# Attention, two mixtures of experts on one core: whole tiles in the gathering, gate values behind places, and a new order of steps in the second mixture

## The chip, the core and the metric

One core of a Trainium2 chip runs the whole program. The time is the device time of one execution in microseconds, and the median over several runs counts. Five engines work side by side: TensorE (matrix products), VectorE, ScalarE, GpSimd and SyncE, called PE, DVE, ACT, POOL and SP in the profile. SyncE here only issues transfers, in order.

## The reference

```python
def reference(**kwargs):
    attn_out = _attn_ref(q, k, v, s)                      # (2, 8, 576, 64): causal, with a decay bias from cumsum(max(s, 0))
    x = attn_out.transpose(0, 2, 1, 3).reshape(1152, 512)
    x = _moe_ref(x, w_gate, w1, w2, capacity=288)         # first mixture: each token to its best of 8 experts
    return _moe2_ref(x, w_gate2, w1b, w2b)                # second: greedy by logit, 144 tokens per expert
```

The bias of a score is `-(cum[i] - cum[j])`, clipped at zero, before the softmax. In the first mixture a token goes to the expert with the largest logit and is scaled by its softmax probability; an expert takes its first 288 tokens. In the second, pairs of token and expert are taken in falling order of their logits, and each expert is full at 144 tokens. An expert computes `relu(x @ w1) @ w2` with w1 of 512 x 1024 and w2 of 1024 x 512.

## The kernel before, in words

The order of the work is written out by hand: no scheduler moves an instruction, and each engine takes its own in program order. Weights and activations are split into a high half in 16 bits and a low half (the rest), so that three products of halves stand for one in 32 bits.

**Attention** runs over 16 heads (two batches of eight), in pairs. A loop `m` from -7 to 18 (line 745) runs a software pipeline: in one turn head `m` gets its exponentials (`E0` to `E3`, line 515) and the halves `ph` and `pl` of its probabilities (`P0`, `P1`, line 536), head `m - 1` its products with v (`V0` to `V2`, `R0` to `R2`), head `m + 3` its row maxima (`M0` to `D3`, lines 464 and 481) and the reference level that is subtracted in the exponent (`G0` and `G1`, lines 488 and 492), pair `m / 2 + 3` its q in 16 bits (`QS`, line 419, whose copy `QD` is line 423). Names and order of a turn are the two lists `ORDER` (line 740). `ENG` (line 391) says by name which engine does a copy: D for VectorE, A for ScalarE, P for GpSimd. The helpers `copied` and `less` carry lines 398, 400, 402 and 411 for all of them. When a pair has its output, `X1` (line 593) makes its two halves in the rows XR, `X` transposes them, `XE` copies them out and `XG` multiplies them with the gate's weights; `LG` adds the logits.

**The gate.** `gate(b)` (line 653) takes the logits of a batch: the maximum, which expert it is (a one-hot `OH`), the exponentials for the gate value, a matmul with a triangle of ones that counts each token's place at its expert, then `sl`, the row of the token in the list `xd` in DRAM, and a scatter of the rows by GpSimd (line 688). For the second batch `slf` is its place within the first expert. The first expert's input is not read back from DRAM only: `first_pe0` (line 628) puts the first batch's part into four banks, and `first_pe1` (line 634) adds the second batch's tokens by a product of XR with one-hots `oh0` of places (line 637: five VectorE operations, one for each 128 tokens, the last of 64). Forty matmuls (line 642) give XA, copied out by ScalarE and VectorE in turn (line 644). `warmer` (line 648) issues matmuls whose results are not used; `WARM` says how many.

**First mixture.** From line 1274 on, eight experts in an order of their sizes. Weights come from DRAM by SP (line 128), are split by ScalarE (line 160, high) and VectorE or GpSimd (line 164, low), in steps put between the matmuls. `split_next` does one quarter of a matrix. Four such quarters, the first expert's first matrix, are split during attention's end: `SPA` (line 698) gives one after each of the turns 13 to 15, line 819 one more, and two of their low halves are GpSimd's (`POOL0`). The load of the second expert's first matrix goes into the same buffer, when all four are split.

**Second mixture.** `phases` (line 1686) finds in up to seven rounds which tokens the next full expert gets, in steps that end with `yield`, while the experts already known are computed. The strings `FIRST` and `THEN` (line 1871) say what stands between an expert's matmuls at each of 22 places: `h` and `l` a high and a low half of a weight split, `w` the next step of `phases`, `s` and `t` the transposes of the next expert's input (`spread`, line 1407), `0` and `1` the two halves of the previous expert's output. `checks` (line 1760) makes sums over the result, from which the kernel decides at the end whether to route again.

## Time and profile before

| | |
|---|---|
| median of 3 runs | 489.27 us (487.54 to 490.25) |
| the profiled execution | 487.02 us, its span 485.2 us |
| PE busy | 413.0 us, 85% of the span |
| DVE busy | 321.1 us, 66% |
| ACT busy | 244.4 us, 50% |
| POOL busy | 190.3 us, 39% |
| DRAM | 81.42 MB read, 14.59 MB written, 198 GB/s over the span |

The span runs from the first to the last instruction; what lies around it makes up the rest of the execution. Attention fills the span up to about 150 us, the first mixture 163 to 280, the choice of the second mixture's tokens up to 326, the second mixture the rest. A share of the whole span is a mean over these, so the rows below are by stretch.

### The profile page before, as it was taken

How to read it: one execution, taken by the hardware profiler on the slowest of the kernel's cores; microseconds unless marked ns; L12 is line 12 of the kernel's file. 1: busy time of each engine (PE TensorE's matmuls, PEld its weight loads, DVE VectorE, ACT ScalarE, POOL GpSimd, SP SyncE). 2: the span in 40 equal slices, each digit the busy share in tenths (PEclk: the TensorE clock that was granted, in tenths of full speed). 3: DMA queues.
4: the chain of work that ended last, by engine and by line, in shares of the span. 5: the costliest groups of instructions: out<-in, count | busy, mean ns of one | idle time of the engine just before them, and what ended most of it. 6: DMA issues, size and time to landing. Idle time of an engine off the chain costs nothing. (4 is left out here: it accounts for less than half of the span.)

```text
span 485.2 us, 13714 instructions
## 1 busy us (share of the span) xinstructions
PE 413.0 (85%) x5227; PEld 380.5 (78%) x5227; DVE 321.1 (66%) x949; ACT 244.4 (50%) x441; POOL 190.3 (39%) x299
## 2 busy tenths in 40 slices
PE   1679999977987999999999985649999999998980
PEld 1557778766774799999999985639899899998980
DVE  6799999995865357777778935458773763653300
ACT  3466777743662246545667604225456456454420
POOL 3595667756743503212322700432233322332211
PEclk9999999987987699999999988657999999999995
DMA  8787889749903689999996910449999769689001
GB/s 174 167 202 168 206 194 223 139 139 313 263 3 127 204 238 387 341 345 391 343 344 139 179 25 7 133 121 273 362 333 340 233 192 353 230 287 309 15 26 29
DMA packets 94405, 103.09 MB, mean 212 GB/s; under 512 B 56136, under 2 KB 63304, under 8 KB 94323
## 3 DMA queue, kind: packets, MB, share of 16 engines
q1 hardware_dynamic: 88931, 91.85, 65.3%
q0 software_dynamic: 4192, 9.91, 6.3%
q8 instruction: 45, 0.74, 0.6%
q10 hardware_dynamic: 1200, 0.30, 0.3%
q14 instruction: 37, 0.30, 0.2%
HBM read 81.42 MB, written 14.59 MB: 198 GB/s over the span
## 5 line engine op out<-in xcount | busy, mean ns | idle before, releaser
L164 DVE TENSOR_TENSOR wl<-wf,wh 128x1024 bf16<-128x1024 f32 x62 | 74.7, 1222 | 19.7 <-ACT wh L160 17.5
L160 ACT ACTIVATE wh<-wf 128x1024 f16<-128x1024 f32 x64 | 65.8, 1050 | 12.3 <-DMA wf<-in_moe_w_dram 12.3
L906 PE MATMUL A<-xt,wl 128*128 128x144 f16 (+4 forms) x288 | 61.0, 235 | 0.0
L905 PE MATMUL A<-xt,wh 128*128 128x144 f16 (+4 forms) x288 | 61.0, 235 | 0.0
L904 PE MATMUL A<-xt,wh 128*128 128x144 f16 (+4 forms) x288 | 61.0, 235 | 0.0
L1074 POOL DMA_INDIRECT x2d<-xo,tix x16 | 26.3, 1646 | 81.7 <-DVE l L1090 33.9
L961 PE MATMUL C<-h,wf 128*128 128x160 f32 (+7 forms) x544 | 58.3, 269 | 0.0
L906 PEld LDWEIGHTS <-wl 128*128 128x128 bf16 x512 | 51.8, 101 | 2.6 <-issue 2.6
L904 PEld LDWEIGHTS <-wh 128*128 128x128 f16 x512 | 51.9, 101 | 1.4 <-PE pM L642 1.4
L905 PEld LDWEIGHTS <-wh 128*128 128x128 f16 x512 | 51.7, 101 | 0.9 <-issue 0.4
L534 ACT ACTIVATE pf<-pE,XB 128x512 f32<-128x512 f32 (+4 forms) x80 | 36.9, 514 | 19.7 <-PE pE L529 15.5
L1815 POOL DMA_INDIRECT out_dram<-x2f,tok x14 | 15.7, 1121 | 66.9 <-ACT h L915 37.5
L411 POOL TENSOR_TENSOR pl<-pf,ph 128x512 f16<-128x512 f32 x30 | 35.2, 1186 | 14.3 <-DVE ph L400 12.6
L961 PEld LDWEIGHTS C<-h,wf 128*128 128x128 f32 x256 | 36.2, 190 | 0.0
L1795 PE MATMUL C<-h,wf 128*128 128x144 f32 x256 | 35.3, 290 | 0.0
L485 DVE CUSTOM_DVE_ANT_0 junk<-pM,cb 128x128 f16<-128x128 f32 (+4 forms) x80 | 32.1, 428 | 3.7 <-PE pM L475 3.6
L473 PE MATMUL pM<-al,ar 128*128 128x128 f16 (+2 forms) x96 | 27.4, 326 | 8.0 <-DVE rm L485 5.1
L1795 PEld LDWEIGHTS C<-h,wf 128*128 128x128 f32 x256 | 32.4, 190 | 0.0
L1399 POOL DMA_INDIRECT xg<-x2d,tok x16 | 22.6, 1411 | 22.1 <-PE A L1117 7.2
L557 PE MATMUL pog<-vf,pf 128*128 128x65 f32 x180 | 30.0, 291 | 0.0
L904 PE MATMUL C<-xt,wh 128*128 128x144 f16 x128 | 25.7, 232 | 0.0
L905 PE MATMUL C<-xt,wh 128*128 128x144 f16 x128 | 25.7, 232 | 0.0
(404 smaller groups left out, 1186.9 us busy)
## 6 DMA issues: line engine op xcount, KB each, us to landing
wf<-in_moe_w_dram SPq DMA_DIRECT2D x128, 512.0 KB
xd<-zero SPq DMA_DIRECT2D x18, 257.0 KB
cb<-cumd SPq DMA_DIRECT2D x16, 288.0 KB
x2d<-zero SPq DMA_DIRECT2D x9, 260.5 KB
kf<-in_k_dram SPq DMA_DIRECT2D x16, 128.0 KB
vf<-in_v_dram SPq DMA_DIRECT2D x16, 128.0 KB
qf<-in_q_dram SPq DMA_DIRECT2D x14, 128.0 KB
bl<-al SPq DMA_DIRECT2D x16, 72.0 KB
```

What stands on the lines that cost most here:

```text
L160: nc.scalar.activation(hi, src, AF.Copy)
L164: (nc.gpsimd if i == 0 and (0, part) in POOL0 else nc.vector).tensor_sub(lo, src, hi)
L411: (nc.gpsimd if ENG[name][i % 2] == "P" else nc.vector).tensor_sub(o, x, y)
L473: nc.tensor.matmul(o, AR[m][:, t * P:(t + 1) * P], AL[m][:, j0:j1], start=True, stop=not diag)
L485: nc.vector.tensor_tensor_reduce(junk[:w, :j1 - j0], o, CB[m][:w, j0:j1], 1.0, r if t == 4 and j0 == 0 else -3e38, OP.add, OP.max, r)
L534: nc.scalar.activation(d, o, AF.Exp, bias=x, scale=2.0 ** -13)
L557: nc.tensor.matmul(o, pf[:, c:c + P], VF[n % 4][:, j, h], start=False, stop=j == t)
L904: nc.tensor.matmul(ph[:, g], wh[:, c, fs], xt[:, c], start=c == 0, stop=False)
L905: nc.tensor.matmul(ph[:, g], wh[:, c, fs], xt[:, 4 + c], start=False, stop=False)
L906: nc.tensor.matmul(ph[:, g], wl[:, c, fs], xt[:, c], start=False, stop=c == 3)
L961: nc.tensor.matmul(py[:, g], a[:, f, d], b[:, f], start=k == 0, stop=k == len(terms) - 1)
L1795: nc.tensor.matmul(py[:, g], a[:, f, d], b[:, f], start=k == 0, stop=k == len(terms) - 1)
```

## The change

In attention's loop the scaling of the row maxima (`q_dve0`) goes from VectorE to ScalarE, with the constant MAGIC as a bias from a tile; the subtraction in `q_dve1` goes from VectorE to GpSimd, and MAGIC is now in `refb`, which VectorE writes; the copy `QD` goes from GpSimd to VectorE. At attention's end: `X1` of pair 6 runs at the end of turn 14 and no longer in turn 15, turn 16 begins with `X` and `XE`, two splits go from before the gate into `first_pe1`, all low halves are VectorE's, the gathering takes five whole tiles (the last filled up with zeros), gate values and the scatter come after the places and one-hots, and the numbers of warming matmuls and their places differ. In the second mixture the strings and one `yield` differ.

```diff
--- before.py
+++ after.py
@@ -78,7 +78,6 @@
     wsp0 = ctx.enter_context(tc.tile_pool(name="wsp0", bufs=1))
     WSP = [tuple(wsp0.tile([P, 4096], t, name=f"{n}{i}") for n, t in (("wh", F16), ("wl", BF16))) for i in range(2)]
     WS = {}
-    POOL0 = ((0, 1), (0, 3))
     ROWS = ('DA', 'DD')
 
     FILL = ". ff ffff ff rf f f rff ff . . . r rf ff fffffff"
@@ -161,7 +160,7 @@
 
     def split_lo(i, part):
         src, hi, lo = split_parts(i, part)
-        (nc.gpsimd if i == 0 and (0, part) in POOL0 else nc.vector).tensor_sub(lo, src, hi)
+        nc.vector.tensor_sub(lo, src, hi)
 
     def split_w(i, part):
         split_hi(i, part)
@@ -327,7 +326,10 @@
 
     g1 = sp.tile([P, S], F32, name="g1")
     XB = ap.tile([P, NT, NH], F32, name="XB")
+
     refb = ap.tile([P, NH, G], F32, name="refb")
+    magic = ap.tile([P, 1], F32, name="magic")
+    nc.vector.memset(magic, MAGIC)
 
     def groups():
         nc.vector.tensor_scalar(g1[64:96], gi[64:96], 0.0, -1024.0, op0=OP.is_ge, op1=OP.mult)
@@ -357,7 +359,7 @@
             nc.tensor.matmul(pr[:, h], selc[:, h:h + 1].to_broadcast([64, P]), refh, start=True, stop=True)
         nc.scalar.activation(XB[:, :4], pb[:, :4], AF.Copy, scale=2.0 ** -13)
         nc.scalar.activation(XB[:64, 4], pb[:64, 4], AF.Copy, scale=2.0 ** -13)
-        nc.scalar.activation(refb, pr, AF.Copy)
+        nc.vector.tensor_scalar(refb, pr, MAGIC, None, op0=OP.add)
 
 
     wgh = const.tile([P, 4, 2, E], F16, name="wgh")
@@ -389,7 +391,7 @@
     later = []
 
     ENG = dict(KL="DD", QL="DD", BR="DD", AL="AA", AR="AA", XE0="AA", XE1="AA", XH="AA",
-               XL="PP", NH="PP", NL="PP", KH="AA", QH="AA", QD="PP", last="DD", PH0="DD", PH1="DD", PL0="PP", PL1="PP",
+               XL="PP", NH="PP", NL="PP", KH="AA", QH="AA", QD="DD", last="DD", PH0="DD", PH1="DD", PL0="PP", PL1="PP",
                VS="DD", VL="PP", VH="AA")
 
     def copied(name, i, o, x, scale=None):
@@ -486,17 +488,16 @@
                                            r if t == 4 and j0 == 0 else -3e38, OP.add, OP.max, r)
 
     def q_dve0(m):
+
         rm = RMS[m % 4]
-        nc.vector.tensor_scalar(rm[:, :NT], rm[:, :NT], 2.0 ** -10, MAGIC, op0=OP.mult, op1=OP.add)
+        nc.scalar.activation(rm, rm, AF.Identity, bias=magic, scale=2.0 ** -10)
 
     def q_dve1(m):
         n, h, b, hh = heads(m)
-        rm = RMS[m % 4]
         qb = QB[n % 3]
         ng = aw.tile([P, NT, G], F32, name="ng")
-        nc.vector.scalar_tensor_tensor(ng, rm[:, :NT, None].to_broadcast([P, NT, G]), MAGIC,
-                                       refb[:, m, None, :].to_broadcast([P, NT, G]),
-                                       op0=OP.subtract, op1=OP.subtract)
+        nc.gpsimd.tensor_tensor(ng, RMS[m % 4][:, :NT, None].to_broadcast([P, NT, G]),
+                                refb[:, m, None, :].to_broadcast([P, NT, G]), OP.subtract)
         copied("NH", m, qb[:, :, h, 64:64 + G], ng)
         less("NL", m, qb[:, :, h, 96:96 + G], ng, qb[:, :, h, 64:64 + G])
 
@@ -631,35 +632,46 @@
             pxa.append(pool.tile([P, 512], F32, name=name)[:, :2 * CA].rearrange("p (c n) -> p c n", c=2))
             nc.tensor.matmul(pxa[k], ident, XA0[:, 2 * k:2 * k + 2], start=True, stop=False, skip_group_check=True)
 
+    oh0s = []
+
+    def first_ones():
+        oh0 = aw.tile([P, NT, 2, 2 * D], F16, name="ka").rearrange("p t h d -> p t (h d)")[:, :, :CA]
+        nc.gpsimd.memset(oh0[64:, 4], 0.0)
+        oh0s.append(oh0)
+
     def first_pe1():
-        oh0 = aw.tile([P, NT, 2, 2 * D], F16, name="ka").rearrange("p t h d -> p t (h d)")[:, :, :CA]
+        oh0 = oh0s[0]
         for t, w in TW:
             nc.vector.tensor_scalar(oh0[:w, t], iota0[:w], slf[:w, t:t + 1], None, op0=OP.is_equal)
+        gate_rows(1)
         for k in range(4):
             for c in range(2):
                 d = 2 * k + c
-                for t, w in TW:
-                    nc.tensor.matmul(pxa[k][:, c], XRP[1][:w, 1, t, d * P:(d + 1) * P], oh0[:w, t], start=False,
+                for t in range(NT):
+                    nc.tensor.matmul(pxa[k][:, c], XRP[1][:, 1, t, d * P:(d + 1) * P], oh0[:, t], start=False,
                                      stop=t == NT - 1, skip_group_check=True)
             (nc.vector.tensor_copy if k % 2 else nc.scalar.copy)(XA[:, 2 * k:2 * k + 2], pxa[k])
-
-    WARM = (4, 4, 2, 2, 4, 4)
+            if k in (0, 2):
+                split_next()
+
+    WARM = (4, 4, 2, 2, 10, 8, 8)
 
     def warmer(k):
 
         for _ in range(WARM[k]):
             nc.tensor.matmul(pog[:, :256], ident, XRP[1][:, 0, 0, :256], start=True, stop=True)
+
+    gates1 = {}
 
     def gate(b):
         lg = LG[:, b]
         g = aw.tile([P, 5, NT], F32, name="gg")
         t3 = aw.tile([P, 3, NT, E], F32, name="gt3")
+        gates1[b] = g, t3
         bc = lambda a: a[:, :, None].to_broadcast([P, NT, E])
         nc.vector.reduce_max(g[:, 0], lg, axis=AX.X)
         nc.vector.tensor_tensor(t3[:, 0], lg, bc(g[:, 0]), OP.is_ge)
-        nc.vector.tensor_tensor(t3[:, 1], lg, bc(g[:, 0]), OP.subtract)
         nc.vector.tensor_tensor(t3[:, 0], t3[:, 0], erev[:, None, :].to_broadcast([P, NT, E]), OP.mult)
-        nc.scalar.activation(t3[:, 1], t3[:, 1], AF.Exp, scale=1.0 / (SX * SG))
         nc.vector.reduce_max(g[:, 1], t3[:, 0], axis=AX.X)
         nc.vector.tensor_tensor(OH[:, b, :4], t3[:, 0, :4], bc(g[:, 1])[:, :4], OP.is_equal)
         nc.vector.tensor_tensor(OH[:64, b, 4], t3[:64, 0, 4], bc(g[:, 1])[:64, 4], OP.is_equal)
@@ -672,18 +684,25 @@
         for t in range(NT - 1):
             mm.append((ones, OH[:, b, t, None, :].to_broadcast([P, NT - 1 - t, E]), t + 1))
         for i, (l, r, t) in enumerate(mm):
+            if b and i == b * NT:
+                warmer(4)
             nc.tensor.matmul(pr[:, t:], l, r, start=i == 0, stop=i == len(mm) - 1, skip_group_check=True)
-        nc.vector.reduce_sum(g[:, 2], t3[:, 1], axis=AX.X)
-        nc.vector.tensor_scalar(g[:, 2], g[:, 2], 1e-9, None, op0=OP.add)
-        nc.vector.reciprocal(xrf[:, b * NT:(b + 1) * NT, 0], g[:, 2])
+        nc.vector.tensor_tensor(t3[:, 1], lg, bc(g[:, 0]), OP.subtract)
+        nc.scalar.activation(t3[:, 1], t3[:, 1], AF.Exp, scale=1.0 / (SX * SG))
         nc.vector.tensor_tensor(t3[:, 2], pr, OH[:, b], OP.mult)
         nc.vector.reduce_sum(g[:, 3], t3[:, 2], axis=AX.X)
         nc.vector.tensor_scalar(g[:, 4], g[:, 3], float(CAP), 1e6, op0=OP.is_ge, op1=OP.mult)
         nc.vector.scalar_tensor_tensor(g[:, 3], g[:, 1], -float(CAP), g[:, 3], op0=OP.mult, op1=OP.add)
-        sl = const.tile([P, NT], I32, name=f"slot{b}")
         if b:
             nc.vector.scalar_tensor_tensor(slf, g[:, 3], e0off, g[:, 4], op0=OP.add, op1=OP.add)
+
+    def gate_rows(b):
+        g, t3 = gates1[b]
+        sl = const.tile([P, NT], I32, name=f"slot{b}")
         nc.vector.scalar_tensor_tensor(sl, g[:, 3], float(E * CAP), g[:, 4], op0=OP.add, op1=OP.add)
+        nc.vector.reduce_sum(g[:, 2], t3[:, 1], axis=AX.X)
+        nc.vector.tensor_scalar(g[:, 2], g[:, 2], 1e-9, None, op0=OP.add)
+        nc.vector.reciprocal(xrf[:, b * NT:(b + 1) * NT, 0], g[:, 2])
         for t, w in TW:
             i = nc.gpsimd.indirect_dma_start(
                 out=xd[:, :], out_offset=bass.IndirectOffsetOnAxis(ap=sl[:w, t:t + 1], axis=0),
@@ -695,7 +714,7 @@
     def rows_x(e, s0, N):
         return slice(e * CAP + s0, e * CAP + s0 + N) if isinstance(e, int) else bass.ds(e * CAP + s0, N)
 
-    SPA = {13: 1, 14: 1, 15: 1}
+    SPA = {13: 1, 14: 1}
 
 
     cnt = const.tile([P, E], F32, name="cnt")
@@ -786,13 +805,23 @@
                              ("L", 9, load_pair), ("LV", 6, load_v), ("XG", -4, lambda n: make("XG", x_pe, n)),
                              ("LG", -4, lambda n: use("XG", lg_add, n))):
             pair_task(name, off, f)
-        for name in ORDER[m % 2]:
+        names = ORDER[m % 2]
+        if m == NH:
+
+            names = ["X", "XE"] + [x for x in names if x not in ("X", "XE")]
+        for name in names:
+            if m == NH - 1 and name == "X1":
+                continue
             if name in tasks:
                 tasks[name]()
                 if m == NH and name in ("V2", "XG"):
                     warmer(name == "XG")
+        if m == NH - 2:
+            x1(NPAIR - 2)
+            first_ones()
         if "LG" in tasks and m == 2 * NP + 2:
             gate(0)
+            gate_rows(0)
             first_experts()
         if m == -5:
             references()
@@ -816,14 +845,13 @@
             nc.sync.dma_start_transpose(XA0, xd.bitcast(F16)[rows_x(order[0], 0, CA), :2 * DM])
         for _ in range(SPA.get(m, 0)):
             split_next()
-    split_next()
     first_pe0()
-    warmer(4)
     gate(1)
     pc = psT.tile([P, S], F16, name="pT").bitcast(F32)[:, :B * NT * E]
     nc.tensor.matmul(pc, ones, OH.rearrange("p b t e -> p (b t e)"), start=True, stop=True)
     warmer(5)
     first_pe1()
+    warmer(6)
     nc.vector.reduce_sum(cnt, pc.rearrange("p (c e) -> p e c", e=E), axis=AX.X)
     nc.vector.scalar_tensor_tensor(key, cnt, float(E), erev, op0=OP.mult, op1=OP.add)
     nc.vector.tensor_tensor(key, key, taken, OP.subtract)
@@ -1761,6 +1789,7 @@
 
         nc.gpsimd.tensor_tensor(chk[:, 0], own0[:, 0], own0[:, 0], OP.mult)
         nc.gpsimd.tensor_tensor(chk[:, 1, :CT], SL2, SL2, OP.mult)
+        yield
         nc.vector.reduce_sum(Q[:, 0, :E], chk[:, 0].rearrange("p t e -> p e t"), axis=AX.X)
         nc.vector.reduce_sum(Q[:, 1, :E], chk[:, 1, :CT].rearrange("p t e -> p e t"), axis=AX.X)
         nc.vector.reduce_sum(dbl[:, 0], BA0, axis=AX.X)
@@ -1868,8 +1897,8 @@
 
 
 
-    FIRST = "w h lw l . 0ww ww . . . . w . ww h . l h wst lh lw1 hll"
-    THEN = "w . . . 0 . . ww . w h l1w h wl . h l . swh tl l ."
+    FIRST = "w h wl l . w . w w w w . w . wh l w h st lh wl hll"
+    THEN = "w . . . 0 w w . w . h w1l h wl h . w l s tl h l"
     FIRST, THEN = (x.split() for x in (FIRST, THEN))
     next(work)
     pop_lo()
```

## Rows read from the trace of the kernel before

**Rows 1.** Busy time by stretch: length, busy us (instructions) per engine, clock, DMA share, GB/s
```profile
17.00:40.00 23.00, 15.85 (x166) 11.56 (x165) 22.04 (x73) 11.95 (x25) 17.85 (x61) 0.93 0.83 199
40.00:100.00 60.00, 57.21 (x818) 48.08 (x818) 59.55 (x199) 45.02 (x96) 40.50 (x49) 1.00 0.82 181
153.00:166.00 13.00, 11.20 (x69) 7.48 (x67) 4.51 (x22) 0.85 (x2) 8.03 (x20) 0.50 0.72 250
166.00:262.00 96.00, 96.00 (x1112) 95.04 (x1109) 69.60 (x126) 54.96 (x93) 24.60 (x33) 1.00 1.03 326
```

**Rows 2.** Groups of instructions by line and form, 40 to 100 us
```profile
L490 DVE TENSOR_SCALAR rm<-rm 128x5 f32<-128x5 f32 x9 | 9.3, 1036 | 0.0
...
L497 DVE SCALAR_TENSOR_TENSOR ng<-rm,refb 128x90 f32<-128x90 f32 x9 | 2.2, 244 | 0.1
...
L400 DVE CAST ph<-pf 128x512 f16<-128x512 f32 x17 | 9.1, 555 | 0.0
...
L400 POOL COPY qa<-qa 128x640 f16<-128x640 f16 x4 | 2.9, 717 | 0.0
...
L411 POOL TENSOR_TENSOR qb<-ng,qb 128x90 f16<-128x90 f32 x9 | 3.2, 352 | 0.7
```

**Rows 3.** Timeline at 74 us: start, us, engine, line, operation
```profile
74.68 1.16 POOL L411 TENSOR_TENSOR pl<-pf,ph 128x512 f16<-128x512 f32 x1 [0.43 <-DVE rs L568]
74.75 1.12 DVE L490 TENSOR_SCALAR rm<-rm 128x5 f32<-128x5 f32 x1
```

**Rows 4.** Timeline of attention's end, 138 to 163 us
```profile
138.35 1.90 DVE L411 TENSOR_TENSOR pl<-pf,ph 128x512 f16<-128x512 f32 x1
...
140.62 0.69 DVE L411 TENSOR_TENSOR pl<-pf,ph 128x512 f16<-128x512 f32 x1
...
142.56 1.27 PE L449 MATMUL pT<-ident,XR 128*128 128x128 f16 x10
...
150.17 1.51 DVE L659 TENSOR_TENSOR gt<-LG,gg 128x40 f32<-128x40 f32 x1
...
151.60 0.19 DVE L660 TENSOR_TENSOR gt<-LG,gg 128x40 f32<-128x40 f32 x1
...
153.97 0.94 DVE L637 TENSOR_SCALAR ka<-iota,slf 128x160 f16<-128x160 f16 x5
...
154.79 1.01 POOL L688 DMA_INDIRECT xd<-XR,slot  x1 [3.18 <-DVE ka L637]
...
155.01 0.64 PEld L642 LDWEIGHTS <-XR 64*128 64x128 f16 x5 [0.29 <-issue]
...
156.26 0.42 ACT L644 CAST XA<-pE 128x320 f16<-128x320 f32 x1 [4.20 <-PE pE L642]
...
162.00 0.49 DVE L644 CAST XA<-pM 128x320 f16<-128x320 f32 x1 [3.46 <-PE pM L642]
...
162.78 0.29 PE L904 MATMUL A<-XA,wh 128*128 128x160 f16 x1 [1.20 <-DVE cnt L827]
```

**Rows 5.** The two halves of a weight split (the page's groups), and SP's load at 151.65
```profile
L164 DVE TENSOR_TENSOR wl<-wf,wh 128x1024 bf16<-128x1024 f32 x62 | 74.7, 1222 | 19.7 <-ACT wh L160 17.5
...
L160 ACT ACTIVATE wh<-wf 128x1024 f16<-128x1024 f32 x64 | 65.8, 1050 | 12.3 <-DMA wf<-in_moe_w_dram 12.3
...
151.65 1.97 SPq L128 DMA_DIRECT2D wf<-in_moe_w_dram  x4
```

**Rows 6.** TensorE's waits from 326 us: us in total, times, longest us
```profile
PE A L1117 <- ACT xt L1420: 2.2, 3, 0.7
...
PE px L1394 <- DVE tot L1736: 1.1, 4, 0.3
...
PE px L1733 <- DVE own L1723: 0.8, 1, 0.8
...
PE D L905 <- DVE xt L1420: 2.3, 1, 2.3
```

**Rows 7.** The table load of ScalarE, all of the execution
```profile
L288 ACT ACT_TABLE_LOAD  x1: 1283/1283/1283, 2.5 to 2.5; - x1
```

## The prediction

> **What bounds the kernel now.** I read the busy time by stretch first [rows 1]. From 40 to 100 us, where nine heads of attention run, VectorE is busy 59.55 of 60 us and TensorE 57.21. Both look full, but only VectorE is: TensorE's short matmuls are counted with their latency, so its row overstates it. VectorE sets the pace there. It does so from 17 to 40 us as well, 22.04 of 23 us, where TensorE has 15.85. From 166 to 262 us, the first experts, TensorE is busy 96.00 of 96 us at the full clock and waits for nothing, so whatever starts this stretch sooner ends it sooner. In between lies the end of attention. From 153 to 166 us TensorE's granted clock is 0.50, which is 1.2 GHz, although the engine is counted busy for 11.20 of 13 us.
>
> Next come the lines of the stretch 40 to 100 [rows 2]. L490 is a VectorE operation on 5 numbers per partition and takes 1036 ns on average. In order of time [rows 3] it starts at 74.75, while GpSimd works from 74.68 to 75.84, and ends just after it: it waits for GpSimd. The Trainium skill (SBUF — State Buffer, section "SBUF: two separate sides") says that VectorE in a two-port mode and GpSimd share one port pair under an exclusive lock, so that one fully blocks the other. The trace agrees with it here: 1.12 us for 5 numbers.
>
> Then the end of attention in order of time [rows 4]. The same subtraction `pl` costs 1.90 us beside GpSimd and 0.69 us without. In the gate, L659 takes 1.51 us on 40 numbers beside GpSimd's split, and its neighbour L660, of the same form, takes 0.19. At L642 the row of one batch's weight loads shows an idle gap of 0.29 us ahead of a load of 64 rows; there are eight such loads, the later ones with 0.25. The experts start at 162.78. Last, TensorE's waits in the second mixture [rows 6].
>
> **Part 1, attention's body (lines 490, 497, 403, 360).** L490 leaves VectorE for ScalarE, L497 leaves it for GpSimd, and the copy QD comes from GpSimd to VectorE. In 40 to 100 us VectorE loses 9.3 + 2.2 = 11.5 us [rows 2]. It gains four copies QD. No row shows this copy on VectorE: the cast of 512 numbers there, 0.56 us on average, bounds it from below (it can't bring a gain), L490 beside GpSimd, 1.12 us, from above. I take 1.0, near the upper end, because QD directly follows the second `ph` and GpSimd starts its `pl` at that moment. So 4 us come back and VectorE is relieved of 7 to 8 us. GpSimd stays level: nine subtractions of about 0.35 us (its row for the same 90 numbers, `qb`) against four copies of 0.72. ScalarE gets about 0.25 us per head at 45.02 us of 60 busy [rows 1]. The next limit is TensorE: the page leaves it 2.8 us of idle in this stretch, and its gaps hidden behind counted latency are some more. I take 3. New waits: L485's last part (t = 4) now waits for ScalarE's version of L490. Ahead of that on ScalarE are two exponentials that were ready earlier, and reciprocal and normalization cover it on VectorE: nothing.
> The other seven of the 16 heads lie in 17 to 40 us, where VectorE is the bound too, and after 100 us. At the rate of the nine, 3 x 7/9 would be 2.3; I take 2.2. Sum: 5.2 us, bounds 1 (the lock moves on) and 9 (VectorE's relief counts whole).
>
> **Part 2, the end of attention.** (a) Moving x of pair 6 forward and `wl` of part 1 to VectorE takes GpSimd out from under the last `pl`: 1.90 - 0.69 = 1.2 us [rows 4]. ScalarE now has the cast of x and a split (1.05 us [rows 5]) in front of head 15's first exponential, and VectorE a split of 1.22, which eats 0.7 of it. The ten transposes of 1.27 us, now between the last V matmuls, go into TensorE's wait for `pl`, and the rest of V then runs less often at the low clock. I take 2.0 (0.5 to 3). (b) In the gate L659 drops by 1.51 - 0.19 = 1.3 us; the integer slots and the subtraction leave the chain (0.1 each). The ten warming matmuls stand ahead of the counting ones and may make these wait some 0.2 us. 1.4. (c) The first one-hot starts at 153.97 and the experts at 162.78: 8.8 us, in which forty matmuls of 160 columns run at 1.2 GHz with eight short weight loads among them. With whole tiles the gaps go (8 x 0.25 = 2 us), and at 2.4 GHz forty take 40 x 0.067 = 2.7 us, an estimate from columns and clock. TensorE would be done about 3.5 us after the first one-hot. But the two splits now lie in this chain on VectorE: five one-hots 0.94, last matmuls and latency 0.5, the XA copy 0.42, the high half 1.05 and low half 1.22 of the first split [rows 5], the second XA copy 0.49, the second low half 1.22, the last XA copy 0.49, and from its end to the experts' start 0.29 as now. Sum 6.6. So 8.8 - 6.6 = 2.2, bounds 1.0 (clock at 1.2 GHz throughout) and 3.9 (the clock is also kept through the first layer). (d) Batch 1's scatter is issued after gate values and one-hots. Its first start now is 154.79, 0.8 us after the one-hots begin. Later it has the one-hots (0.94) and four small operations like L660 (0.19 each) in front of it, so about 2.4: 1.6 more, on a start that (a) and (b) put 3.4 earlier. The loads behind it on SP, expert 1's rows and its second weights, still come 1.8 us sooner than now. Expert 1's first weights, at 151.65 now, wait for the last low half: 153.97 - 3.4 + 5.8 = 156.4, about 4.7 us later against the trace. I cost both at nothing, because expert 1's turn is a whole expert later; this is rival 3. Sum 5.6 us, bounds 2.5 and 8.
>
> **Part 3, the second mixture.** The transposes of a row of maxima (`w`) go ahead of the spreading (`s`), whose bank they wait for: three waits, 2.2 us. The counts go ahead of the low half (`l`): four waits, 1.1 us. The paired `ww` are pulled apart: 0.8. A yield between GpSimd's squares and VectorE's sums lets VectorE copy xt meanwhile: 2.3 us [rows 6]. That is 6.4 us on the engine that is the bound. High halves move later by a step or two, and something will wait anew: I take 5.8, bounds 2 and 6.4.
>
> **Sum.** 5.2 + 5.6 + 5.8 = 16.6 us. The profiled execution took 487.02 us (span 485.2), 2.25 below the median of the runs, 489.27. The experts' stretches follow TensorE, so I carry the sum over whole: 470.4 for that execution, 472.7 for the median.
>
> **Rivals.** 1: the lock moves. The same section of the Trainium skill speaks against the change: it counts every operation of two SBUF inputs among those that the lock stops, so the low halves that come to VectorE too. By rows, as a mechanism of this kernel: QD meets GpSimd's `pl` at 1.1 us, and the casts `ph` and `br` take what L490 waited before. The body then gives 1 instead of 5.2: 476.9. For it, 1.90 against 0.69 for one and the same operation [rows 4]; against it, L490 sits where GpSimd always works, the others often don't. Chance 0.2. 2: the clock. In 153 to 166 us it is 0.50 although TensorE has much to do there. If it falls during the 2 to 3 us in which TensorE waits for the splits, or before the gathering, part 2 gives 2.5: 475.8. Chance 0.2. 3: expert 1's weights come late and ScalarE's splits hold up the relus: up to the 4.7 us of the delay are lost, 477.4. Against it, TensorE waits for no weights now. Chance 0.1. 4: the waits of the second mixture only change place: 2 instead of 5.8, 476.5. Chance 0.12. 5, slower: the bias form on ScalarE (Identity) belongs to another table than Exp. Then each head loads tables twice, 2 x 1.283 [rows 7] = 2.6 us. ScalarE has 45.02 / 9 = 5.0 us per head in a period of 6.7; with 0.25 and 2.6 it has 7.8 and sets the pace, 1.1 us more per head or 18 for 16. It decides once ScalarE's head exceeds 6.7 us. 489.3 + 18 - 11.4 = 496. Against it: Exp and the copying form alternate in this trace with one load in all. Chance 0.03. The Trainium skill (ScalarE: Activation LUTs, "Table sets: the hidden batching unit") says that identity is in every set; by that the loads don't come. No run here shows it yet.
>
> **How the numbers follow.** The forecast has the remaining 0.35. 472.7 is the likeliest. Upper bounds of all parts together, 9 + 8 + 6.4 = 23.4, give 466; two rivals at once, 4.2 and 3.8 less, give 480.7. Range 466 to 481 leaves out the table case and three rivals at once. A measurement tells 0.5%, 2.4 us, from no change. All cases but the fifth are faster by more: faster 0.95, same 0.02, slower 0.03.
>
> **What would show it.** VectorE's row in 40 to 100 below 9.6 of 10, L490 on ScalarE near 0.25 us, heads closer by some 0.4 us; L659 near 0.2; no idle gaps at L642, its matmuls at clock 1.0; the first expert's matmul about 6.5 us after the first one-hot; waits at L1117, L1394, L1733 and L905 gone after 320 us. Wrong: heads no closer, QD near 1 us with `ph` longer, clock 0.50 at L642, TensorE waiting for wh of expert 1, or table loads in the loop.

## The result, and the profile after

The changed kernel takes **471.34 us** (median of 4 runs, 470.20 to 472.17); the kernel before, run beside it, 488.40 (4 runs, 485.78 to 490.25). The ratio is 0.9653, with a 95% interval from 0.9601 to 0.9705. The forecast of 472.7 is met within 1.4 us. Its sum is not: attention's heads gave more than their term (1.6 to 5.8 us more, as one counts heads 10 to 12 below), and expert 0 took 5.7 us that had been costed at nothing. The rest of this document is mostly about these two.

The profiled execution of after took 471.41 us, with a span of 469.5 (before 487.02 and 485.2). To see where the 15.7 us lie, both timelines are cut at the first instruction of a stage. The same cuts are used for every kernel run here. In the columns: from the start of the program to head 0 (its exponential of the last 64 rows), heads 0 to 10, 10 to 12, 12 to 15, from there to the first one-hot, the gathering up to the first expert's matmul, expert 0, expert 1, the rest of the first mixture up to the spreading, the ranking up to the counting, from there to the second mixture's first layer, and from there to the end of the span. Every number is a difference of two starts in the timeline.

```
kernel         start  heads  heads  heads   gate gather expert expert   rest ranking to 2nd  2nd to   span
                       0-10  10-12  12-15                    0      1                layer     end
before          31.9   68.2   22.8   15.2   15.9    8.8   17.0   15.5   92.0   20.2   19.4  158.3   485.2
after           33.3   61.4   18.6   15.7   11.9    6.5   22.7   15.4   89.5   20.5   20.6  153.4   469.5
body_only       32.6   61.9   18.2   15.2   16.5    8.3   16.9   15.4   89.4   18.9   20.8  160.1   474.2
round_only      31.9   66.5   18.1   15.8   14.5    8.4   17.1   15.4   92.0   18.2   20.1  160.2   478.2
qd_pool         34.4   61.8   21.4   16.0   12.0    6.5   22.2   15.5   89.3   20.5   19.5  152.7   471.8
end_only        34.5   67.5   23.2   16.7   12.0    6.4   21.2   15.4   92.0   20.5   19.6  161.9   490.9
early_splits    33.1   61.4   18.7   15.6   12.4    4.5   15.3   20.8   89.3   20.2   19.5  153.2   464.0
relus_first     32.9   61.5   18.6   15.7   12.0    6.4   15.4   22.5   89.6   20.5   19.4  153.0   467.5
both_relus      34.0   61.5   23.0   15.6   11.9    6.5   15.4   20.2   89.6   16.5   19.6  153.7   467.5
early_relus     33.9   61.4   18.6   15.7   12.3    4.5   15.4   15.9   90.1   22.1   19.5  152.8   462.2
partial_tiles   33.8   61.5   22.9   15.6   12.4    5.9   16.7   15.4   89.4   16.7   19.3  153.6   463.2
few_warm        33.8   61.5   22.9   15.6   12.3    4.5   17.1   15.4   89.7   18.3   19.5  153.4   464.0
late_only       33.2   68.1   22.7   16.1   14.4    8.5   17.1   15.4   90.1   19.7   19.3  152.8   477.4
yield_only      34.1   67.6   24.3   15.1   14.5    8.8   16.9   15.5   90.0   19.6   19.4  156.0   481.8
```

Read the columns before the rows. Four of them move between kernels that don't differ there: the start (31.9 to 34.5), heads 10 to 12 (18.6 to 22.9 in kernels that are the same up to there), the rest of the first mixture (89.3 to 92.0) and the ranking (16.5 to 22.1). A cause is read from the other columns. Where the code is the same, heads 0 to 10 and the gathering repeat within 0.7 us, the others within about 2. (The profile of end_only is of a slower execution, 492.88 us beside its median of 487.10.) By these columns attention's heads 0 to 10 give 6.8 us, gate and gathering 6.3, the last stage 4.9, and expert 0 **takes back 5.7**. Heads 10 to 12 give 4.2 more in this pair; how much of that is the edits' isn't settled (last section).

Busy time by stretch of after, columns as in [rows 1]; the third and fourth are the gathering and expert 0, the last the part of expert 0 behind its hole:

```profile
17.00:40.00 23.00, 15.78 (x157) 11.67 (x155) 20.83 (x66) 12.38 (x28) 19.07 (x63) 0.85 0.81 190
40.00:95.00 55.00, 55.00 (x824) 47.63 (x823) 51.92 (x186) 45.94 (x106) 45.21 (x54) 1.00 0.91 203
141.00:147.40 6.40, 4.21 (x48) 3.48 (x47) 4.80 (x15) 2.77 (x4) 3.52 (x3) 1.00 0.22 85
147.40:170.10 22.70, 18.19 (x161) 17.46 (x162) 9.53 (x17) 7.80 (x12) 8.06 (x21) 0.85 0.95 250
159.30:165.00 5.70, 5.70 (x23) 5.22 (x24) 5.56 (x5) 4.54 (x7) 2.75 (x3) 0.58 0.89 282
```

Expert 0 in before, the same columns:

```profile
162.78:179.83 17.05, 17.05 (x160) 17.02 (x161) 9.49 (x17) 7.97 (x12) 2.17 (x11) 0.90 0.69 171
```

In 40 to 95 us VectorE has 3.1 us of slack, and TensorE is counted busy for the whole stretch with 824 matmuls, 15.0 per us; before it had 818 in 60 us [rows 1], 13.6. So TensorE could run 10% more work in a time that was already counted 95% busy. The gathering runs at the full clock (0.50 in [rows 1]). The row of expert 0 has the new hole: 4.5 us of 22.7 idle. Behind it TensorE's granted clock is 0.58, and 0.85 over the whole expert. An expert 0 that nothing stops takes 15.4 us at the full clock (four kernels below), so the 22.7 are these 15.4, 4.5 of idle and some 2.8 of clock. Before's 17.0 have no idle, and some 1.6 of clock at 0.90.

Groups of instructions by line and form, 40 to 95 us, of after:

```profile
L402 DVE CAST ph<-pf 128x512 f16<-128x512 f32 x18 | 10.4, 598 | 0.0
...
L499 POOL TENSOR_TENSOR ng<-rm,refb 128x90 f32<-128x90 f32 x9 | 3.5, 393 | 0.5 <-DVE rm L487 0.5
...
L493 ACT ACTIVATE rm<-rm,magic 128x5 f32<-128x5 f32 x9 | 2.7, 299 | 0.9 <-DVE rm L487 0.6
...
L402 DVE COPY qa<-qa 128x640 f16<-128x640 f16 x4 | 1.3, 314 | 0.0
```

The rounding costs 0.30 us on ScalarE (1.04 on VectorE [rows 2]), the subtraction 0.39 on GpSimd, and the copy QD 0.31 on VectorE, where the forecast took 1.0: it starts 0.2 us ahead of GpSimd's `pl` and not behind it (46.48 and 46.70 us in the first of the four, the others alike). The cast `ph` went from 0.555 to 0.598.

Attention's end in order of time, of after, with SP's load of expert 1's first matrix:

```profile
138.45 0.20 DVE L673 TENSOR_TENSOR gt<-LG,gg 128x40 f32<-128x40 f32 x1
...
140.95 0.94 DVE L645 TENSOR_SCALAR ka<-iota,slf 128x160 f16<-128x160 f16 x5
...
141.27 1.27 PE L651 MATMUL pE<-ka,XR 128*128 128x160 f16 x10 [0.56 <-DVE ka L645]
...
145.53 1.22 DVE L163 TENSOR_TENSOR wl<-wf,wh 128x1024 bf16<-128x1024 f32 x1
146.66 0.48 DVE L653 CAST XA<-pM 128x320 f16<-128x320 f32 x1
...
146.77 2.46 SPq L127 DMA_DIRECT2D wf<-in_moe_w_dram  x4
...
147.44 0.23 PE L932 MATMUL A<-XA,wh 128*128 128x160 f16 x1 [1.96 <-DVE cnt L855]
...
149.42 0.44 ACT L943 ACTIVATE h<-A 128x320 f32<-128x320 f32 x1 [4.08 <-PE A L934]
157.86 1.06 ACT L159 ACTIVATE wh<-wf 128x1024 f16<-128x1024 f32 x1 [8.00 <-DMA wf<-in_moe_w_dram]
158.83 0.42 ACT L943 ACTIVATE h<-A 128x320 f32<-128x320 f32 x1
...
159.30 10.94 PE L989 MATMUL C<-h,wf 128*128 128x160 f32 x60 [4.47 <-ACT h L943]
```

The `is_ge` of the gate takes 0.20 us (1.51 in [rows 4]). From the first one-hot to the experts it is 6.5 us, and the chain is the one that the forecast wrote down: the last low half at 145.53, the last copy of XA at 146.66, the first expert's matmul. The same low half releases the load: SP issues it at 146.77, 0.7 us before expert 0 begins. Before, it was issued at 151.65 [rows 5], 11.1 us ahead of expert 0 at 162.78 [rows 4]. Now ScalarE evicts the first part of h at 149.42, reaches a high half of expert 1 and stands there for 8.00 us until the matrix has landed. The other three evictions of h stand in the same queue behind it, and TensorE waits 4.47 us for them.

TensorE's waits of after from 306 us on, columns as in [rows 6], all but the smallest:

```profile
PE A L1446 <- DMA xg<-x2d,tok: 6.0, 2, 4.8
PE px L1568 <- ACT g L1560: 1.2, 4, 0.3
PE C L934 <- DVE wl L163: 1.2, 1, 1.2
PE D L1840 <- ACT x2f L1842: 1.1, 1, 1.1
PE A L1145 <- DVE m L1709: 0.9, 1, 0.9
```

The first and the last of these lie ahead of the second mixture's first layer, and before has both too, ahead of 326 us (4.5 and 0.9 us). The four waits of [rows 6], 6.4 us, are gone. New ones have come: 1.2 us for `wl`, the high halves that moved later, and 1.2 us in four parts for `g`.

### The profile page after: what moved, and what is told of

Read it like the earlier page. It is cut to its first block, busy times and chain, and to the rows that moved or that the text cites. A ratio compares the mean times of both kernels' runs of the same rounds, so it can differ in the third digit from the quotient of the medians.

```text
span 469.5 us, 13728 instructions
## 1 busy us (share of the span) xinstructions
PE 400.9 (85%) x5245; PEld 374.5 (80%) x5245; DVE 310.2 (66%) x929; ACT 246.6 (53%) x456; POOL 193.0 (41%) x306
## 5 line engine op out<-in xcount | busy, mean ns | idle before, releaser
L163 DVE TENSOR_TENSOR wl<-wf,wh 128x1024 bf16<-128x1024 f32 x64 | 77.9, 1235 | 26.4 <-ACT wh L159 24.8
L989 PE MATMUL C<-h,wf 128*128 128x160 f32 (+7 forms) x544 | 61.1, 274 | 4.5 <-ACT h L943 4.5
L1102 POOL DMA_INDIRECT x2d<-xo,tix x16 | 27.9, 1743 | 79.4 <-DVE l L1118 31.3
L933 PE MATMUL A<-xt,wh 128*128 128x144 f16 (+4 forms) x288 | 59.5, 231 | 0.0
L932 PE MATMUL A<-xt,wh 128*128 128x144 f16 (+4 forms) x288 | 59.5, 231 | 0.0
L932 PEld LDWEIGHTS <-wh 128*128 128x128 f16 x512 | 50.7, 99 | 2.2 <-issue 2.2
L933 PEld LDWEIGHTS <-wh 128*128 128x128 f16 x512 | 50.5, 99 | 0.9 <-issue 0.4
L1844 POOL DMA_INDIRECT out_dram<-x2f,tok x14 | 17.4, 1244 | 62.7 <-ACT h L943 35.8
L989 PEld LDWEIGHTS C<-h,wf 128*128 128x128 f32 x256 | 38.2, 199 | 5.2 <-ACT h L943 5.2
L1824 PEld LDWEIGHTS C<-h,wf 128*128 128x128 f32 x256 | 32.5, 190 | 0.8 <-ACT h L943 0.8
L1427 POOL DMA_INDIRECT xg<-x2d,tok x16 | 20.8, 1300 | 22.1 <-PE C L1824 6.3
L934 PE MATMUL C<-xt,wl 128*128 128x144 f16 x128 | 24.9, 228 | 1.2 <-DVE wl L163 1.2
L932 PE MATMUL C<-xt,wh 128*128 128x144 f16 x128 | 25.0, 228 | 0.0
```

The source lines that it names most:

```text
L163: nc.vector.tensor_sub(lo, src, hi)
L932: nc.tensor.matmul(ph[:, g], wh[:, c, fs], xt[:, c], start=c == 0, stop=False)
L933: nc.tensor.matmul(ph[:, g], wh[:, c, fs], xt[:, 4 + c], start=False, stop=False)
L934: nc.tensor.matmul(ph[:, g], wl[:, c, fs], xt[:, c], start=False, stop=c == 3)
L989: nc.tensor.matmul(py[:, g], a[:, f, d], b[:, f], start=k == 0, stop=k == len(terms) - 1)
L1102: i = nc.gpsimd.indirect_dma_start(out=x2d[:, :], out_offset=bass.IndirectOffsetOnAxis(ap=t, axis=0), in_=xo, in_offset=None, bounds_check ...
```

## Experiments

The four kernels of the first comparison take one part each of the change, or put its splits elsewhere. The times of before beside them: 486.24 us, 13 runs.

**Part 1 alone (body_only).** The kernel before with

```diff
...
-        nc.scalar.activation(refb, pr, AF.Copy)
+        nc.vector.tensor_scalar(refb, pr, MAGIC, None, op0=OP.add)
...
-QD="PP"
+QD="DD"
...
-        nc.vector.tensor_scalar(rm[:, :NT], rm[:, :NT], 2.0 ** -10, MAGIC, op0=OP.mult, op1=OP.add)
+        nc.scalar.activation(rm, rm, AF.Identity, bias=magic, scale=2.0 ** -10)
...
-        nc.vector.scalar_tensor_tensor(ng, ...)
+        nc.gpsimd.tensor_tensor(ng, ..., OP.subtract)
```

> The kernel before with part 1 alone (MAGIC in the references, the rounding on ScalarE, the subtraction on GpSimd, QD on VectorE). Forecast's step: 5.2 us faster than before, 483 (ratio 0.989). Theory now (VectorE's relief counts whole, because QD costs 0.3 us there and not 1.0): the last exponential of head 15 comes 8 to 9 us sooner and the time is 8 to 10 us lower, 478 to 480 (0.980 to 0.984). Rival 1 (the lock moves on): 487 or more.

474.38 us (471.81 to 476.46), ratio 0.9738 (0.9668 to 0.9809): 12 us faster, more than any theory. Heads 0 to 10 take 61.9 us, 6.3 less than before; heads 10 to 12 take 18.2 and not 22.8. The first is the edits'. For the second the last section shows two causes, of which the edits remove one.

**Part 2 alone (end_only).** The kernel after, with the edits of body_only and of part 3 taken back:

```diff
-        nc.scalar.activation(rm, rm, AF.Identity, bias=magic, scale=2.0 ** -10)
+        nc.vector.tensor_scalar(rm[:, :NT], rm[:, :NT], 2.0 ** -10, MAGIC, op0=OP.mult, op1=OP.add)
...
-    FIRST = "w h wl l . w . w w w w . w . wh l w h st lh wl hll"
+    FIRST = "w h lw l . 0ww ww . . . . w . ww h . l h wst lh lw1 hll"
```

> The kernel before with part 2 alone (all edits between head 13 and the first expert). Forecast's step: 5.6 us faster, 483. Theory now: the first expert's first matmul comes 5 to 6 us sooner, and expert 0 then takes 5 to 6 us longer because the first matrix of expert 1 is asked for later and its splits sit on ScalarE ahead of the relus: the time is 0 to 1 us lower than before (ratio 0.998 to 1.000), and expert 1 starts where it does now, within 1 us. If rival 3 were not the cause of expert 0's 22.7 us, expert 0 takes its 17 us here and the time is 483.

487.10 us, ratio 1.0001 (0.9963 to 1.0038): nothing. The gathering takes 6.4 us as in after, expert 0 takes 21.2. In the trace ScalarE is seen to stand for the load again, with the evictions of h between the high halves (timeline of end_only, ScalarE):

```profile
163.05 0.44 ACT L943 ACTIVATE h<-A 128x320 f32<-128x320 f32 x1 [4.81 <-PE A L934]
169.82 1.06 ACT L159 ACTIVATE wh<-wf 128x1024 f16<-128x1024 f32 x1 [6.33 <-DMA wf<-in_moe_w_dram]
170.78 0.42 ACT L943 ACTIVATE h<-A 128x320 f32<-128x320 f32 x1
```

The part that was written for the end of attention gives back in expert 0 what it gains before it.

**Part 3 alone (late_only)**, the two strings and the `yield` of the diff:

```diff
-    FIRST = "w h lw l . 0ww ww . . . . w . ww h . l h wst lh lw1 hll"
-    THEN = "w . . . 0 . . ww . w h l1w h wl . h l . swh tl l ."
+    FIRST = "w h wl l . w . w w w w . w . wh l w h st lh wl hll"
+    THEN = "w . . . 0 w w . w . h w1l h wl h . w l s tl h l"
```

> The kernel before with part 3 alone (the two strings and the yield). Forecast's step: 5.8 us faster, 482.6. Theory now, from the stretches of the kernel after: 5 us, 483.4 (ratio 0.990). Rival 4 (waits only change place): 2 us, 486.4. If the late part only came out better because the first part ended sooner, less than 2.

479.59 us, ratio 0.9862 (0.9805 to 0.9918). From the second mixture's first layer to the end 152.8 us instead of 158.3: **5.5 us**, beside the forecast's 5.8. The column itself is not that sharp: it is 158.3, 160.1 and 160.2 in before, body_only and round_only, which have the same code there, and 152.7 to 153.7 in the kernels with all of part 3, so the part is worth some 5 to 7 us.

**The splits ahead of the gate (early_splits).** In after:

```diff
-    SPA = {13: 1, 14: 1}
+    SPA = {13: 1, 14: 1, 15: 1, 16: 1}
...
-            if k in (0, 2):
-                split_next()
```

> The kernel after, but the last two splits of expert 0's first matrix stand behind heads 15 and 16 of the loop, ahead of the gate, and not in the gathering; all low halves stay on VectorE. Theory now (rival 3: the last low half releases the load of expert 1's first matrix, and everything behind it is late): the load is issued some 8 us sooner, expert 0 takes 17 to 18 us instead of 22.7, and the gathering loses its two splits: 5 to 8 us under the kernel after, 463 to 466 (ratio to before 0.949 to 0.955). If the splits cost the same wherever they stand and expert 1 is late for another reason: 471, like the kernel after. If the splits ahead of the gate hold the end of attention by their whole 2 x 1.2 us and the load gains nothing: 473.

466.25 us, ratio 0.9573 (0.9510 to 0.9637), faster than both kernels. The gathering falls to 4.5 us and expert 0 to 15.3. But expert 1 rises from 15.4 to 20.8. The trace of early_splits (SP's load of expert 1's first matrix, ScalarE in expert 1, and TensorE's wait):

```profile
135.88 1.97 SPq L127 DMA_DIRECT2D wf<-in_moe_w_dram  x4
...
172.17 1.06 ACT L159 ACTIVATE wh<-wf 128x1024 f16<-128x1024 f32 x1 [3.38 <-DMA wf<-in_moe_w_dram]
173.13 0.42 ACT L941 ACTIVATE h<-A 128x320 f32<-128x320 f32 x1
...
PE C L987 <- ACT h L941: 2.2, 1, 2.2
```

The load is issued 9.8 us ahead of expert 0 again. The same trap now stands one expert later: the first high half of expert 2 in front of the last eviction of expert 1.

The second four ran beside a before of 487.24 us (7 runs).

**Evictions first, load still late (relus_first).** In after:

```diff
+    STEPS.update({(0, 0): '', (0, 1): '', (0, 2): '', (0, 3): 's s s s'})
```

> The kernel after, with the load of expert 1's first matrix as late as it is there, but the four high halves of that matrix stand on ScalarE behind the last relu of expert 0 instead of between its relus. Theory now (what was lost in expert 0 is the relus standing in ScalarE's queue behind a high half that waits for its load): TensorE's wait of 4.5 us for h is gone, expert 0 takes 16.5 to 18 us instead of 22.7, the first mixture ends 4 to 6 us sooner and the time is 465 to 467 (ratio to before 0.955 to 0.960). Rival (the lateness of the matrix itself bounds expert 1, wherever the halves stand): expert 1's first matmul stays at 170 within 1 us and the time is 470 to 471.

467.96 us, ratio 0.9579 (0.9523 to 0.9635). Expert 0 falls to 15.4 us as the theory has it, but expert 1 takes 22.5. The two together take 37.9 us, against 38.1 in after. Neither theory holds whole: expert 1 starts sooner, at 162.5 and not at the rival's 170, but the rival was right about the sum. The queue on ScalarE decided in *which* expert the late matrix was paid; expert 1's own evictions still stand behind a high half that waits, and both_relus, further on, takes that away too. The 3 us between the medians of after and relus_first come from two comparisons, and the stages don't show them.

**The same for expert 1, with the early load (early_relus).** In early_splits:

```diff
+    STEPS.update({(1, 2): '', (1, 3): 's s'})
```

> The kernel early_splits, with the first high half of expert 2's first matrix moved behind the last relu of expert 1. Theory now: the 3.8 us by which early_splits ended the first mixture ahead of the kernel after, although it started expert 1 9 us ahead, are what is left because the same queueing comes back one expert later (TensorE's wait of 2.2 us for h); with the relu first that wait goes, and the time is 1.5 to 4 us under early_splits, 462 to 465 (0.950 to 0.955). Rival (the stream of weights, with the DMA engines full from 161 us, bounds the experts): 466, like early_splits, with the wait moved to wl or wh.

463.45 us, ratio 0.9502 (0.9429 to 0.9576). Experts 0 and 1 take 31.3 us together, and no wait for h is left among TensorE's in the first mixture (the longest two):

```profile
PE D L1092 <- DVE l L1097: 1.2, 2, 0.8
PE px L1228 <- DVE lg L1222: 0.6, 1, 0.6
```

This is the fastest version, some 8 us under after by medians from two comparisons. What follows expert 1 keeps its pace (90.1 us), so the stream of weights does not bound it.

**The rounding alone (round_only).** In before:

```diff
...
-        nc.vector.tensor_scalar(rm[:, :NT], rm[:, :NT], 2.0 ** -10, MAGIC, op0=OP.mult, op1=OP.add)
+        nc.scalar.activation(rm, rm, AF.Identity, bias=magic, scale=2.0 ** -10)
```

> The kernel before with one move alone: the rounding of the five maxima (L490, 1.04 us a head) from VectorE to ScalarE. If this operation's waiting for GpSimd is what the body lost (and the other VectorE operations do not take the wait over), 7 to 11 us faster than before, 475 to 479 (0.978 to 0.985), most of what the body's edits together gave (12). If the wait passes to the next VectorE operation (rival 1), under 3 us: 483 or more. If only the three moves together relieve VectorE, about a half, 480 to 482.

482.13 us, ratio 0.9887 (0.9825 to 0.9948). By the time alone the theory of a half fits. The stages say otherwise: heads 0 to 10 take 66.5 us, only 1.0 to 1.7 less than the four kernels without the edits (67.5 to 68.2). What else it gained stands mostly in heads 10 to 12, 18.1 us, where the four kernels have 22.7 to 24.3. Why the ten heads gained so little is in the row of a later VectorE operation, the subtraction `ng` (L497 before; minimum, median and maximum in ns, 40 to 95 us), and in order of time, with what GpSimd does beside one of the long ones:

```profile
L499 DVE SCALAR_TENSOR_TENSOR ng<-rm,refb x9: 236/632/1453, 43.4 to 94.9; 128x90 f32<-128x90 f32 x9
...
54.19 2.36 POOL L413 TENSOR_TENSOR XR<-xs,XR 128x640 f16<-128x640 f32 x1
55.21 1.45 DVE L499 SCALAR_TENSOR_TENSOR ng<-rm,refb 128x90 f32<-128x90 f32 x1
```

It took 0.244 us on average before [rows 2]. With the rounding gone, it meets what GpSimd does after `pl`, and ends just behind it: the low half of XR in four of the nine (0.98 to 1.45 us), the copy QD in three (0.63 each). In sum `ng` takes 7.7 us (2.2 before), and the 17 casts `ph` 0.618 each (0.555 before): together 6.6 of the 9.3 us that the rounding had cost have come back. VectorE is full again:

```profile
40.00:95.00 55.00, 53.29 (x771) 44.94 (x770) 54.07 (x180) 45.14 (x100) 42.91 (x45) 1.00 0.83 188
```

**QD back on GpSimd (qd_pool).** In after:

```diff
-QD="DD"
+QD="PP"
```

> The kernel after with the copy QD back on GpSimd, nothing else. Theory now: GpSimd, which has the subtraction in addition, is full again (45.2 + 4 x 0.72 of 55 us) and its operations are the ones that wait; VectorE gets 0.31 us a pair back. 1 to 4 us slower than the kernel after, 472 to 475. The forecast's price of 1.0 us for QD on VectorE would make it 0 to 3 us faster. If neither engine bounds the heads now and TensorE does: 471, no change.

473.95 us, ratio 0.9718 (0.9659 to 0.9776), which overlaps with that of after. Heads 0 to 10 take 61.8 us against 61.4: the place of QD is worth at most 0.4 us there. Its heads 10 to 12 take 21.4 us, and in that column kernels with the same code differ by more, so the median settles nothing.

The last four ran beside a before of 488.53 us (13 runs).

**Evictions first in both experts, load late (both_relus).** In after:

```diff
+    STEPS.update({(0, 0): '', (0, 1): '', (0, 2): '', (0, 3): 's s s s', (1, 2): '', (1, 3): 's s'})
```

> The kernel after with its late load, and the high halves behind the last relu in expert 0 (as in relus_first) and in expert 1 (as in early_relus). It tells the queue on ScalarE from the lateness of the load. Experts 0 and 1 together took 38.1 us in the kernel after, 37.8 in relus_first and 31.3 in early_relus. Theory A (only the queueing costs): 31 to 33 us here, the first mixture ends at 260 to 261, 5 to 6 us under the kernel after. Theory B (the load is late against TensorE's need, and whatever is let through first waits afterwards): 36 us or more, with TensorE waiting for wl, wh or wf, and at most 2 us under the kernel after.

469.93 us, ratio 0.9635 (0.9603 to 0.9668). Experts 0 and 1 take 35.6 us: between the two theories, nearer to B. Of the 6.8 us that lie between after (38.1) and early_relus (31.3), 2.5 come back with ScalarE's queue in order, and 4.3 go with the lateness of the load. The waits of both_relus have changed their engine (TensorE's waits, 140 to 272 us):

```profile
PE D L1094 <- DVE negi L1086: 1.5, 1, 1.5
PE D L1095 <- DVE y L993: 1.3, 2, 1.1
PE D L1094 <- DVE l L1099: 0.8, 1, 0.8
```

What TensorE needs from VectorE now comes late, behind low halves that stand there one after the other; so the 4.3 hold a queue too, VectorE's (timeline of both_relus, VectorE):

```profile
163.04 4.63 DVE L164 TENSOR_TENSOR wl<-wf,wh 128x1024 bf16<-128x1024 f32 x4 [8.78 <-ACT wh L160]
169.78 1.23 DVE L164 TENSOR_TENSOR wf<-wf,wf 128x1024 bf16<-128x1024 f32 x1 [2.11 <-ACT wf L160]
...
171.02 0.22 DVE L1086 TENSOR_SCALAR negi<-jp 128x128 f16<-128x128 int32 x1
```

**64 rows again (partial_tiles).** In early_relus:

```diff
-                for t in range(NT):
-                    nc.tensor.matmul(pxa[k][:, c], XRP[1][:, 1, t, d * P:(d + 1) * P], oh0[:, t], start=False,
+                for t, w in TW:
+                    nc.tensor.matmul(pxa[k][:, c], XRP[1][:w, 1, t, d * P:(d + 1) * P], oh0[:w, t], start=False,
```

> The kernel early_relus, with the last tile of 64 rows in the gathering's matmuls again (8 loads of 64 rows), nothing else. From the first one-hot to the first expert's matmul early_relus takes 4.5 us at the full clock. If each such load costs the gap of 0.25 us that the kernel before shows: 2 us more, 6.5. If the gaps also bring TensorE's clock down: 8 or more. If the gaps were a consequence of the low clock in the kernel before and not of the 64 rows: 4.5 to 5. Time: 463.5 to 466.

465.59 us, ratio 0.9561 (0.9519 to 0.9604). The gathering takes 5.9 instead of 4.5 us, at the full clock. So eight loads of 64 rows cost 1.4 us, 0.18 each, and don't bring the clock down:

```profile
146.20:152.10 5.90, 5.62 (x48) 3.49 (x48) 2.65 (x13) 0.85 (x2) 2.98 (x3) 1.00 0.51 200
```

**Fewer warming matmuls (few_warm).** In early_relus:

```diff
-    WARM = (4, 4, 2, 2, 10, 8, 8)
+    WARM = (4, 4, 2, 2, 4, 4, 0)
```

> The kernel early_relus, with the warming matmuls of the kernel before in number (4 in the gate instead of 10, 4 behind it instead of 8, none behind the gathering instead of 8), whole tiles kept. If the warming matmuls are what keeps the clock up: the gathering's matmuls take 0.34 us and not 0.23, the way from the first one-hot to the experts grows from 4.5 to 6.5 us and the first layer starts at the lower clock: 2 to 4 us slower. If the whole tiles do it: clock 1.0 as now, and the experts start 0.5 to 1 us sooner, since eight warming matmuls of 1.04 us in all stand ahead of them now.

465.87 us, ratio 0.9576 (0.9518 to 0.9633). The gathering takes 4.5 us at the full clock without the 18 additional matmuls:

```profile
146.10:150.60 4.50, 3.34 (x40) 2.76 (x40) 2.69 (x13) 0.85 (x2) 1.86 (x2) 1.00 0.48 195
```

The experts don't start sooner, and expert 0 takes 17.1 us instead of 15.4, at clock 1.00 but with short stops (0.8 us for `cnt`, the others "issue" by the profile). partial_tiles shows some of these too. So neither the whole tiles nor the warming matmuls are needed for the full clock as long as the other is there. With neither, and with the end of attention as before, the gathering's clock is 0.57 (body_only). What lifts it when both are gone and the rest of part 2 is kept wasn't tried.

**The yield alone (yield_only).**

```diff
         nc.gpsimd.tensor_tensor(chk[:, 1, :CT], SL2, SL2, OP.mult)
+        yield
```

> The kernel before with the yield alone, between GpSimd's squares and VectorE's sums. The forecast's part for it is 2.3 us of the 5.8 (TensorE's wait at L905 for xt): that wait is gone from the list and the time is 1.5 to 2.5 us lower (ratio 0.995 to 0.997), a little over what the runs can tell. If it only changes place: 0. The rest of what part 3 alone gave (6.6 us) then belongs to the two strings.

484.90 us, ratio 0.9936 (0.9915 to 0.9956). From the second mixture's first layer to the end 156.0 us instead of 158.3: 2.3, the length of the wait at L905, which is gone. The other waits of [rows 6] stand as before, in the same lengths. By this pair the strings have the remaining 3.2 of late_only's 5.5; the column differs by 2 us between kernels with the same code, so the wait that is gone says more than the difference.

## Why the prediction was right, and where it was not

**Part 1, mis-sized.** The step that failed is "the next limit is TensorE ... I take 3" for the nine heads. The heads gave about twice that: 6.3 us in heads 0 to 10 of body_only, and the nine kernels in which both operations are moved lie at 61.4 to 61.9. TensorE's row is full there (55.00 of 55 us) and VectorE's isn't, so TensorE may well be the next limit, as the text said; no run shows it apart. The 2.8 us of idle in [rows 1] were no bound, because a busy share that counts the latency of short matmuls hides slack; the text said so and then sized the term by it. The count of matmuls per us would have been no better before the run: it tells what was done and not what could be. For the seven other heads 2.2 was taken; in heads 12 to 15 nothing came, in heads 10 to 12 up to 4.2. By the medians part 1 alone gave 11.9 us, more than the term's upper bound of 9; that bound was meant to count VectorE's relief whole, but 7.5 us in nine heads would be 13 in sixteen.

The price of QD, 1.0, was wrong too (0.31 measured), without weight: the place of QD is worth at most 0.4 us in the heads.

Rival 1, that the lock moves, did not hold for the change as a whole: the cast `ph` grew by 43 ns and the heads are faster. For the rounding alone it held for the most part. The forecast put 9.3 of VectorE's 11.5 us on L490 and 2.2 on L497, and read each as the price of that operation. round_only shows that the wait is no property of the operation: when the rounding goes, `ng` comes to stand beside GpSimd's next work and takes 5.5 us more, `ph` 1.1, and the heads gain 1.0 to 1.7. With `ng` moved too the waits don't pass on. The Trainium skill (SBUF — State Buffer, section "SBUF: two separate sides") counts operations of two SBUF inputs among those that are shut out, and `ng`, at 0.236 to 1.453 us, agrees. What it did not bring is the harm the rival saw for the low halves: their mean went from 1.222 [rows 5] to 1.235 us.

**Part 2, right up to the first expert's matmul.** Items (a) and (b) were 3.4; last head to first one-hot takes 11.9 to 12.0 with the whole of part 2, and 14.4 to 16.5 in the five kernels with the old end, so 2.4 to 4.6. Each of the last two `pl` takes 0.69 us in after (1.90 and 0.69 before), as (a) had it. Item (c) was a way of 6.6 us in place of 8.8: it is 6.5. The gaps of the 64-row loads were 2 us by the forecast and are 1.4 by partial_tiles. The clock is 1.00 there, so rival 2 fell; the clock fell later, behind the hole in expert 0.

**Part 2 (d), wrong.** The step was: "I cost both at nothing, because expert 1's turn is a whole expert later". Rival 3 had the mechanism, ScalarE's splits that hold up the relus, and set it at up to 4.7 us with a chance of 0.1; it cost 5.7, of which 4.5 are TensorE's wait and the rest the lower clock behind it. Two things were missing. The delay was worked out against the trace (151.65 to 156.4) and not against the consumer: the load was issued 11.1 us ahead of expert 0, and the landing takes 10 to 11 us (146.77 to 157.86 in after), so a lead of 0.7 can't do. And the consumer is not expert 1 but the first high half, which stands in expert 0's own queue of evictions. "TensorE waits for no weights now" was true and no evidence, since the lead was being removed. end_only shows what this step did to the part: 5.6 us forecast, none measured.

**Part 3, right.** 5.8 forecast, 5.5 alone and 4.9 within the change. The yield gives 2.3 as its wait said, the strings about 3.2 of 4.1; the new waits for `wl` and `g`, 1.2 us each in after, are what "something will wait anew" allowed for. Rival 4 fell.

**Rival 5** fell: Identity with a bias brings no table load into the loop. The trace of after has one in all, as the Trainium skill (ScalarE: Activation LUTs, "Table sets: the hidden batching unit") says of identity:

```profile
L287 ACT ACT_TABLE_LOAD x1 | 1.3, 1283 | 2.5 <-issue 2.5
```

**The sum** came out by luck: the heads gave more than forecast (6.3 shown, with 4.2 beside it in this pair that may be chance, against 5.2), and expert 0 took 5.7 that had been costed at nothing. A good total was no proof of the steps; early_relus is what the change gives with the second error mended.

## What to carry to other kernels

- When a step moves, follow what its *last* instruction releases. Set the lead of a released load against its landing time, and look for its first consumer in the queue of every engine, not in the stage it is for: an in-order engine makes all that stands behind a waiting instruction late.
- When an operation is slow because of its neighbour on another engine, moving it alone can hand the wait on (here 6.6 of 9.3 us). Ask which operation comes to stand beside that engine's work next, and move the whole group.
- Letting work past a late transfer moves most of the bill to the next stage (both_relus gave 2.5 of 6.8 us) unless the transfer itself comes sooner.
